# Attention scores in 64x64 array tiles without the masked quarter, and paired half blocks, in a planned attention + MLP kernel

## The chip, the cores and the metric

The kernel runs on one core of a Trainium2 chip. A core has five engines that run side by side and wait for one another through semaphores: TensorE (PE in the profile; its weight loads are shown as PEld), VectorE (DVE), ScalarE (ACT), GpSimd (POOL) and SyncE (SP). POOL, SP and ACT also start DMA transfers. The metric is the device time of one execution in microseconds.

## The reference, cut to what matters

```python
batch, n_heads, seq, head_dim = (8, 8, 576, 64)
scores = scale * np.matmul(q, k.transpose(0, 1, 3, 2))
rel = pos[:, None] - pos[None, :]
bias = slopes[:, None, None] * (-np.abs(rel))[None, :, :]
mask = (rel >= 0) & (rel < 128)
scores = np.where(mask, scores + bias[None], -1000000000.0)
attn = softmax(scores)
x = np.matmul(attn, v) -> (4608, 512)
h = x @ w_in           # 512 -> 2048
g = np.maximum(h, 0.0) ** 2
out = g @ w_out        # 2048 -> 512
```

A query sees itself and the 127 keys before it. Rows 128 to 255 of a batch, as an example, see keys 1 to 255: a block of 128 queries needs its own block of keys and the block before. Cut into quarters of 64 keys by 64 queries, the early half of the earlier keys is outside the window for the late queries, and the late half of the own keys lies in the future of the early queries. So one quarter of each of the two 128x128 squares is masked throughout. A batch of 576 rows is four blocks of 128 and a half block of 64.

## The kernel before, in words

All work is written as tasks, each with the engine (or engines) that may run it, an estimate of its time, what it depends on, and which buffer of which ring it takes and frees. `Plan.order` simulates the engines with these estimates and writes the tasks of each engine in one fixed order. The sort key of a task is a due time plus an adjustment from the table `ADJ` (lines 54 to 444), which holds one number for most tasks; the estimates, `SLACK` (line 27) and the `LAND` times of transfers decide when the planner thinks that a task could start. On the chip each engine then runs its list in that order and waits only where a semaphore says so.

**Loads.** `load_block` (line 819) brings k, q and v of one block from DRAM through POOL's DMA queue, turning them to bf16: k and q into a ring `kq` of 4, v into a ring `vt` of 9 (the blocks that start a batch have places of their own, `vf` and `kqf`). `transpose_kq` (line 893) turns k and q over: for the first 8 blocks by TensorE, for the rest by a DMA transpose on SP's queue into a ring `kqT` of 7. There are 40 blocks: 8 first blocks, 24 full ones and 8 half blocks of 64 rows, and each has a `kq`, a `vt` and a `kqT` buffer of its own, the half blocks too. What the 64 rows of a half block leave free in a buffer is set to zero (`zero`, line 784).

**Scores.** `job` (line 937) makes the scores with keys on the partitions and queries along the row. The head dimension is 64, so a matmul uses 64 rows of the array, and two heads run side by side in its two row halves: the profile writes the tile of the array as `64*128`. A full block takes 16 matmuls of 128 keys by 128 queries (8 heads, two squares). A half job handles the half blocks of two batches together: 32 matmuls of 128 keys by 64 queries, with a 64-query part for each batch. The scores lie in four PSUM banks of the ring `a`. ACT takes the exponential of each bank (`expo`, line 1000: four times 512 columns), DVE multiplies by a table of masks that hold the bias and the window (`mask`, line 1007: four times 512 columns). The result is one buffer of the ring `P` of 3. `place(h)` (line 711) says where a head's part lies. The first four blocks go another way (`lone`).

**Values.** `values` (line 1056) multiplies by v, in two bundles of four heads: 8 matmuls of 128x65 each for a full block (two squares), with a column of ones that gives the sum; DVE takes the reciprocal (line 1108) and scales (line 1117) into a buffer of the ring `x`. In a half job this is done once for each of the two batches, 32 matmuls in all, and each writes half of the partitions of one `x` buffer. A DMA transpose on SP's queue puts `x` into `xT`.

**MLP.** Nine groups of 512 rows. The first product goes through `unit` (line 1227), `fc_step` (line 1252) or, from group 6, a Strassen scheme with seven products (`up_product`, line 1313); ACT and DVE do the squared ReLU. The second is direct for group 0 (`o_piece`, line 1406) and a Strassen scheme from group 1 on (`product`, line 1471). PSUM holds two banks `h`, one each `ox` and `oy`, and four `a`. Attention tasks lie between the MLP's matmuls on TensorE until about two thirds of the time; after that only MLP work is left.

`job` gives the planner's cost of the scores, before the change:

```python
t = plan.add({"PE": 213.0 + len(grps) * 2 * len(pieces) * mm(128 if n == 128 else 64)}, due - 32, scores,
```

## Time and profile before

| what | us |
|---|---|
| median of three runs | 299.22 |
| lowest and highest of them | 297.59, 299.52 |
| the profiled execution | 299.3 |
| its span, first to last instruction | 297.4 |
| PE busy in the span | 285.0 |
| DVE busy | 244.0 |
| ACT busy | 205.8 |
| POOL busy | 106.3 |

The profiled execution took 299.3 us, of which 1.9 us lie outside the span; it stands within 0.1 us of the median. The granted clock of TensorE was 1.00 of full speed. A line of the profile such as `L974 PE MATMUL s<-kqT 64*128 64x128 bf16 x192 | 13.3, 216 | 0.0` says: source line, engine, operation, what it writes and reads, the tile of the array, the shape, how many; then the busy time in us, the mean of one in ns, and the idle time of the engine just before them. A matmul's duration runs from its start to its result, and the next one starts long before that, so what a matmul costs a busy TensorE is the distance between the starts, which the timeline gives, and not the duration.

### The profile page before, as it was taken

The page shows a single profiled execution, that of the slowest core. Times are in us where ns is not written, and L with a number is a line of the kernel's source. Part 1 is how long each engine was busy: PE and PEld are TensorE (multiplying, and loading weights), DVE is VectorE, ACT ScalarE, POOL GpSimd, SP SyncE. Part 2 cuts the span into 40 slices and gives each one's busy share as a digit, 9 for nine tenths or more (in the row PEclk, how much of TensorE's full clock was granted, in tenths as well). Part 3 has the DMA queues.
Part 4 walks back from the last instruction along what each step waited for, and adds up shares of the span by engine and source line. Part 5 has one row for each costly group of instructions (what it writes and reads, how often), then busy time and mean ns, then how long its engine had stood idle before and what let it go on. Part 6 is the DMA issues. An engine that isn't in the chain of part 4 may idle for free.

```text
span 297.4 us, 8313 instructions
## 1 busy us (share of the span) xinstructions
PE 285.0 (96%) x3279; PEld 224.4 (75%) x3299; DVE 244.0 (82%) x626; ACT 205.8 (69%) x392; POOL 106.3 (36%) x132
## 2 busy tenths in 40 slices
PE   7899999999998999899999999999999999999994
PEld 3588757888887986457656756768889888888884
DVE  5566568689976996689958997999999998799964
ACT  2785555495496655877679797878999578989600
POOL 8944488452842755441439622710000000000000
PEclk9999999999999999999999999999999999999999
DMA  9999999999999999999999999998212111201124
GB/s 125 168 201 207 184 180 173 155 157 174 163 165 186 161 146 182 158 165 139 155 186 150 148 191 169 165 130 171 68 40 79 53 35 37 71 2 35 31 77 144
DMA packets 170792, 39.62 MB, mean 133 GB/s; under 512 B 156800, under 2 KB 170240, under 8 KB 170752
## 3 DMA queue, kind: packets, MB, share of 16 engines
q0 software_dynamic: 115184, 18.10, 88.9%
q1 hardware_dynamic: 54768, 20.33, 40.0%
q10 hardware_dynamic: 800, 0.66, 0.8%
q8 instruction: 26, 0.43, 0.6%
q14 instruction: 14, 0.11, 0.1%
HBM read 36.70 MB, written 9.44 MB: 155 GB/s over the span
## 4 chain that ended last, share of the span: by engine, by line
PE 69%; DMA 14%; DVE 6%; POOL 4%; issue 3%; ACT 1%; SPq 0%; POOLq 0%; DVEq 0%
PE o L1503 25%; PE h L1259 12%; PE h L1340 10%; PE h L1241 8%; DMA vt<-in_v_dram 5%; PE o L1416 5%; DMA w_out_sb<-in_moe_w_out_dram 4%; PE pv L1089 4%; PE s L974 4%; DMA kqT<-kq 3%; DMA xT<-x 3%; POOL kq L854 2%; POOL vf L859 1%; DVE g L1214 1%; POOL w_in_sb L799 1%
## 5 line engine op out<-in xcount | busy, mean ns | idle before, releaser
L1202 ACT ACTIVATE rt<-h 128x512 bf16<-128x512 f32 (+1 forms) x109 | 64.8, 597 | 32.8 <-PE h L1241 13.9
L1001 ACT ACTIVATE P<-s 128x512 bf16<-128x512 f32 x120 | 63.8, 604 | 7.8 <-PE s L974 7.7
L1503 PEld LDWEIGHTS <-g 128*128 128x128 bf16 x624 | 59.9, 98 | 8.4
L1214 DVE TENSOR_TENSOR g<-rt 128x512 bf16<-128x512 bf16 (+1 forms) x100 | 41.4, 417 | 20.0 <-ACT rt L1202 18.6
L854 POOL DMA_DIRECT2D kq<-in_k_dram x39 | 33.1, 849 | 66.0 <-DMA kqT<-kq 60.7
L1503 PE MATMUL o<-w_out_sb,g 128*128 128x256 bf16 x384 | 47.5, 273 | 0.0
L1241 PE MATMUL h<-xT,w_in_sb 128*128 128x128 bf16 (+1 forms) x512 | 46.2, 246 | 1.0 <-DMA xT<-x 0.9
L1259 PE MATMUL h<-xT,w_in_sb 128*128 128x512 bf16 x178 | 45.5, 379 | 0.7
L1241 PEld LDWEIGHTS <-w_in_sb 128*128 128x128 bf16 x512 | 38.7, 98 | 5.2 <-issue 1.1
L1009 DVE TENSOR_TENSOR P<-P,masks 128x512 bf16<-128x512 bf16 x96 | 38.4, 417 | 2.5 <-ACT P L1001 0.7
L854 POOL DMA_DIRECT2D kq<-in_q_dram x39 | 33.3, 853 | 7.4 <-PE h L1241 3.1
L1117 DVE TENSOR_TENSOR x<-pv,rec 128x256 bf16<-128x256 f32 (+1 forms) x80 | 32.2, 416 | 0.9
L1503 PE MATMUL o<-wsum,sums 128*128 128x256 bf16 x256 | 31.6, 273 | 1.1 <-DVE osb L1561 0.6
L859 POOL DMA_DIRECT2D vt<-in_v_dram x32 | 27.0, 858 | 11.6 <-PE pv L1089 9.8
L1503 PE MATMUL o<-wsum,g 128*128 128x256 bf16 x240 | 29.8, 273 | 0.1
L1089 PEld LDWEIGHTS <-P 128*128 128x128 bf16 x576 | 24.0, 98 | 7.2 <-issue 2.0
L1259 PEld LDWEIGHTS <-w_in_sb 128*128 128x128 bf16 x192 | 16.9, 97 | 15.9
L1212 ACT ACTIVATE g<-rt 128x512 bf16<-128x512 bf16 x45 | 27.9, 629 | 1.1
L1503 PEld LDWEIGHTS <-sums 128*128 128x128 bf16 x256 | 24.4, 98 | 4.8 <-DVE sums L1633 0.6
L1361 DVE TENSOR_TENSOR vf<-h,vf 128x512 f32<-128x512 f32 x36 | 24.1, 683 | 0.8 <-ACT vf L708 0.4
L1202 ACT ACTIVATE rt<-vf 128x512 bf16<-128x512 f32 x36 | 22.2, 624 | 2.4 <-DVE vf L1361 2.2
L1089 PE MATMUL pv<-vt,P 128*128 128x65 bf16 x448 | 22.0, 193 | 1.3 <-DMA vt<-in_v_dram 1.3
(81 smaller groups left out, 382.0 us busy)
## 6 DMA issues: line engine op xcount, KB each, us to landing
out_dram<-osb SPq DMA_DIRECT2D x53, 128.0 KB, 3.8
kq<-in_k_dram POOLq DMA_DIRECT2D x31, 128.0 KB, 7.6
kq<-in_q_dram POOLq DMA_DIRECT2D x31, 128.0 KB, 7.9
vt<-in_v_dram POOLq DMA_DIRECT2D x24, 128.0 KB, 8.0
w_out_sb<-in_moe_w_out_dram POOLq DMA_DIRECT2D x4, 512.0 KB, 14.7
w_in_sb<-in_moe_w_in_dram POOLq DMA_DIRECT2D x3, 512.0 KB, 10.7
vf<-in_v_dram POOLq DMA_DIRECT2D x8, 128.0 KB, 6.9
out_dram<-osb SPq DMA_DIRECT2D x4, 256.0 KB, 6.4
```

The source lines that it names most:

```text
L854: nc.gpsimd.dma_start(view(kq[s_kq[m].idx], i), source(src, m, split))
L859: nc.gpsimd.dma_start(tile_of(s_v[m])[0:n, :, 0:D], source(v, m))
L1001: nc.scalar.activation(flat(Pt[sP.idx]), sS[i].tile.rearrange("p (j t) -> p j t", j=2)[:, :, lo:hi], AF.Exp, bias=0.0, scale=scale)
L1009: nc.vector.tensor_tensor(flat(Pt[sP.idx]), flat(Pt[sP.idx]), flat(masks), op=ALU.mult)
L1089: nc.tensor.matmul(sv.tile[0:full, hi * (D + 1):(hi + 1) * (D + 1)], prob, tile_of(s_v[mk])[:, h, 0:D + 1], start=mk == parts[0][1], stop= ...
L1117: nc.vector.tensor_tensor(o, heads(sv)[rows, :, 0:D], sr.tile[rows, :].unsqueeze(2).to_broadcast([n, 4, D]), op=ALU.mult)
L1202: nc.scalar.activation(srt.tile[:, 0:n], i, AF.Relu, bias=0.0, scale=1.0)
L1214: nc.vector.tensor_tensor(o, i, i, op=ALU.mult)
L1241: nc.tensor.matmul(slot.tile[:, f * w:(f + 1) * w], w_in_sb[:, cc, fc * 128:(fc + 1) * 128], xT[:, cc, lo % (XR * 128):lo % (XR * 128) + w ...
L1259: nc.tensor.matmul(slot.tile, w_in_sb[:, cc, fc * 128:(fc + 1) * 128], xT[:, cc, g * 512 % (XR * 128):g * 512 % (XR * 128) + 512], start=c ...
L1340: nc.tensor.matmul(slot.tile[:, j * 256:j * 256 + 256], a, b_, start=fresh and j == 0 and c == 0, stop=c == 1, skip_group_check=True)
L1503: nc.tensor.matmul(slot.tile[:, z * 256:z * 256 + 256], stationary(c), moving(c), start=fresh and z == 0 and c == 0, stop=c == F - 1, skip ...
```

## The change

For full blocks, only three of the four quarters of each square are computed, each as matmuls of 64 keys by 64 queries: the output goes to half of the partitions of a bank, so the tile is 64*64 and four can be addressed (two row halves for two heads, two column halves for early and late keys). A full block takes 48 such matmuls in place of 16. Two of the four banks hold 512 columns, two hold 256: the third quarters of the two squares share a bank, one on the early partitions and one on the late. ACT's exponentials are two of 512 and two of 256 columns. DVE's mask instruction for the shared quarters reads 64 columns and writes them twice, each time with a mask that zeroes what belongs to the other square.

The half blocks of two batches become one block of 128 rows: loaded into one `kq` and one `vt` buffer by two transfers of 64 rows for each of k, q and v, turned over by one DMA transpose, and handled as one job with one `x` buffer. There are 36 blocks in place of 40. A half job takes 48 matmuls of 64x64 for the scores in place of 32, a second `P` buffer (`sR`) for the later batch's earlier keys, DVE instructions that mask and clear parts (`clear`, `far_late`, `far_early`, `near`), and 24 value matmuls in place of 32 with one set of reciprocals and scalings in place of two. The instructions that zeroed buffer halves go.

The places of the heads change, planner's estimates change (`S_PE`, the slack of v and x, stores, the landing time of loads), and the `ADJ` table is another, so the order of the work is another. On TensorE the first 503 matmuls stand in the same order as before, past the scores of the first two-block job.

```diff
-SLACK = {"kq": 0.0, "kqT": 4500.0, "v": 2000.0, "x": 2500.0}
+SLACK = {"kqT": 4500.0, "v": 2300.0, "x": 2700.0}
+S_PE = 375.0
...
-        jobs.append(("half", [len(seq), len(seq) + 1]))
-        seq += [(b, HALF), (b + 1, HALF)]
+        jobs.append(("half", [len(seq)]))
+        seq.append((b, HALF))
...
     def place(h):
-        return (h // 4) * 4 + (h % 2) * 2 + (h // 2) % 2
+        return (h % 2) * 4 + h // 2
...
                 for i, src in enumerate((k, q)):
-                    nc.gpsimd.dma_start(view(kq[s_kq[m].idx], i), source(src, m, split))
+                    for rows, from_ in sources(src, m):
+                        nc.gpsimd.dma_start(view(kq[s_kq[m].idx], i)[rows], from_)
...
         if kind == "full":
-            pieces = [(part * 128, 128, part, mk, ms[0]) for part, mk in ((0, before[ms[0]]), (1, ms[0]))]
+            banks = [[(mb, whole, 0, early), (me, whole, 64, late)], [(me, early, 0, early), (mb, late, 0, late)]]
+        elif kind == "half":
+            banks = [[(mk, whole, 64 * i, (early, late)[i]) for i, mk in enumerate(before)],
+                     [(me, early, 0, early), (me, late, 0, late)]]
...
+                todo = [(n, c, p) for n, pieces in enumerate(banks) for c in range(C) for p in pieces]
+                for n, c, (mk, keys, at_c, qs) in todo:
+                    mq = mk if diag else me
+                    for half in (early, late) if keys == whole and not diag else (keys,):
+                        for r in range(2):
+                            rows = slice(64 * r, 64 * r + 64)
...
+                                w = (128, 64)[n]
+                                o = sS[2 * r + n].tile[half, c * w + at_c:c * w + at_c + 64]
+                            nc.tensor.matmul(o, tile_of(s_kqT[mk])[rows, c, half],
+                                             tile_of(s_kqT[mq])[rows, C + c, qs], start=True, stop=True)
...
-            t = plan.add({"PE": 213.0 + len(grps) * 2 * len(pieces) * mm(128 if n == 128 else 64)}, due - 32, scores,
+            t = plan.add({"PE": 213.0 + (449.0 if diag else S_PE)}, due - 32, scores,
...
+            cols = 256 if i % 2 and not diag else 512
...
+                if i % 2:
+                    nc.vector.tensor_tensor(p[:, :, 1:3], p[:, :, 2:3].to_broadcast([128, 4, 2, 64]), mk[:, :, 1:3], op=ALU.mult)
                 else:
+                    nc.vector.tensor_tensor(p[:, :, 0:4:3], p[:, :, 0:4:3], mk[:, :, 0:4:3], op=ALU.mult)
...
+        if kind == "half":
+            def clear():
+                nc.vector.memset(Pt[sR.idx][:, :, 0, early], 0.0)
+
+            def far_late():
+                nc.vector.tensor_tensor(Pt[sR.idx][:, :, 0, late], Pt[sP.idx][:, :, 0, late], masks[:, :, 0, early],
+                                        op=ALU.mult)
+
+            def far_early():
+                p = Pt[sP.idx][:, :, 0, early]
+                nc.vector.tensor_tensor(p, p, masks[:, :, 0, early], op=ALU.mult)
+                nc.vector.memset(Pt[sP.idx][:, :, 0, late], 0.0)
+
+            def near(w):
+                p = Pt[sP.idx][:, w, 1].rearrange("p c (s q) -> p c s q", s=2)
+                nc.vector.tensor_tensor(p, p[:, :, 1:2].to_broadcast([128, 4, 2, 64]),
+                                        masks[:, w, 1].rearrange("p c (s q) -> p c s q", s=2), op=ALU.mult)
+                nc.vector.memset(Pt[sP.idx][early, w, 1, late], 0.0)
...
+            parts = [(s, slice(0, 128), mk) for s, mk in zip((sP, sR), before)] + [(sP, slice(128, 256), m)]
```

## The prediction

> **What bounds the kernel now.** I read the page first.

> ```profile
> span 297.4 us, 8313 instructions
> PE 285.0 (96%) x3279; PEld 224.4 (75%) x3299; DVE 244.0 (82%) x626; ACT 205.8 (69%) x392; POOL 106.3 (36%) x132
> ...
> PEclk9999999999999999999999999999999999999999
> DMA  9999999999999999999999999998212111201124
> ```

> TensorE is the bound: 12.4 us of the span are without a matmul, and the clock is full throughout. DMA is as full, but only up to slice 28, about 208 us; after that TensorE works alone. The view by windows puts the 12.4 us in place.

> ```profile
> 0.00:20.00 20.00, 16.15 (x195) 11.05 (x197) 11.94 (x49) 11.43 (x31) 16.31 (x24) 1.00 1.52 162
> 20.00:280.00 260.00, 255.28 (x2958) 201.26 (x2975) 222.04 (x560) 194.30 (x362) 90.01 (x108) 1.00 1.35 133
> 280.00:298.00 18.00, 13.53 (x132) 12.05 (x130) 10.03 (x18) 0.12 (x1) 0.00 (x0) 0.99 0.33 103
> ```

> The second number of PE is busy time: 3.85 us idle in the start, some 3.9 after 280 us (up to the end at 297.4), and 4.72 in between. So the change can win what it takes off TensorE's list, plus at most a part of these 4.72. Which waits they are, the list of waits says:

> ```profile
> POOL vt L859 <- PE pv L1089: 9.8, 3, 6.8
> ...
> PE pv L1089 <- DMA vt<-in_v_dram: 1.3, 1, 1.3
> ...
> PE h L1241 <- DMA xT<-x: 0.9, 1, 0.9
> ```

> The rest are many small ones. What a score burst costs, the timeline of PE shows by the distance of starts, for a full block (first fence) and for a half job (second):

> ```profile
> 59.37 0.23 PE L974 MATMUL s<-kqT,kqf 64*128 64x128 bf16 x2
> 59.43 0.22 PE L974 MATMUL s<-kqT 64*128 64x128 bf16 x2
> ...
> 59.71 0.22 PE L974 MATMUL s<-kqT,kqf 64*128 64x128 bf16 x2
> 59.77 0.22 PE L974 MATMUL s<-kqT 64*128 64x128 bf16 x2
> ```

> ```profile
> 136.49 0.23 PE L974 MATMUL s<-kqT,kqT 64*128 64x64 bf16 x4
> 136.56 0.22 PE L974 MATMUL s<-kqT 64*128 64x64 bf16 x4
> ...
> 136.91 0.22 PE L974 MATMUL s<-kqT 64*128 64x64 bf16 x4
> ```

> Two matmuls of 128 columns start together every 0.056 us (59.37 to 59.77 in 7 steps, rounded starts; 55.7 ns by the full list). Two of 64 columns start together every 29.2 ns (0.42 us for 14 rounds, so 60 ns for the four of a row). A full burst is 8 rounds, 8 x 55.7 = 446 ns; a half burst 16 x 29.2 = 467 ns. Each is preceded and followed by a gap of about 0.1 us when the array changes its tile (the last row's four end their rounds at 136.97, and the next start is at 137.06).

> **The change, part by part.**

> *Scores.* 24 full and 4 half bursts become 48 matmuls of 64 columns in 64*64 tiles. The trace has no such tile. Lower bound: all four tiles work side by side, 48 / 4 = 12 rounds of 29.2 ns = 350 ns. Upper bound: only two work side by side, as in the half burst now, 24 x 29.2 = 701 ns. In the half burst, two matmuls with their two weight loads are issued within 7 ns of a 29.2 ns round by the full list of starts, so twice as many fit into a round (14 of 29), and issue does not forbid four. Each tile now loads 128 columns of weights per round, afterwards 64. I take 350 ns. Saved: 24 x (446 - 350) + 4 x (467 - 350) = 2304 + 468 = 2.77 us. The gaps around the bursts I leave as they are: the array changes its tile at the same places. A gap twice as long at both ends would cost 28 x 0.2 = 5.6 us; one that vanishes would win as much; the row before me is the same gap for another pair of tiles, so nothing.

> [...] The trace shows only that 128 columns load within 29.2 ns in today's tile.

> *Values.* 32 matmuls go (4 pairs x 8), of 30 ns each:

> ```profile
> 143.13 0.97 PE pv L1089 x32
> ```

> (chain of waits: 0.97 us for 32). Saved: 0.97 us, all on TensorE's path.

> *ACT.* 56 exponentials go from 512 to 256 columns: the 512 form has a mean of 604 ns, the 256 form of the relu has 387, so 56 x 0.217 = 12.2 us less of 205.8. ACT is not the bound; I count nothing. If the strided forms cost 30% more than these rows (56 x 0.18 + 56 x 0.12 = 17 us), ACT would stand at 210 us, far below PE.

> *DVE.* A half job: now four masks (415), four reciprocals (171), four scalings (418) = 4.02 us. Then four masks of 512 columns (417), a cleared half of `P` twice (272 by the memset of 64x256), two small clears (165), two reciprocals and two scalings = 1.67 + 0.54 + 0.33 + 1.18 = 3.72 us. Three memsets of 0.7 us in all go. Together some 2 us less of 244. The new mask form reads one operand twice; the row with a repeated operand (L1016) has 415 ns, the dearest row for 512 columns of DVE has 688. At 688 the 56 instructions would cost 15 us more, 257 of 294: still under PE. Nothing counted, with the cover named: TensorE's other work between scores and values.

> *DMA, SP, POOL.* Bytes are the same, POOL's k, q and v transfers are 78 and 40 as before, SP has 28 transposes of `kqT` in place of 32, the four of them twice as tall. A half pair takes one of nine `vt` and one of seven `kqT` buffers in place of two. The one long wait for v (1.3 us) came from a load that POOL could not start until old values had been used (9.8 us in three waits), so this is eased. I credit 0.5 us, between 0 and the 1.3.

> *Order.* By the order of the built kernel the last score burst has 203.7 us of TensorE work before it (now 200.7, in the same prices), though the attention work before it has become 3.9 us less; so some 6.9 us more MLP work stands ahead of it. Last scores would come at 220.5 + 3.2 = 223.7 us: the loads have more time than today, not less. Nothing counted.

> **Sum.** Against the profiled 299.3 (0.1 over the median): 299.3 - 2.77 - 0.97 - 0.5 = 295.1 us. The start's order is the same and the tail is the same chain, so their 7.7 us stay.

> **The rivals.**

> *New waits at the half blocks (no change).* Values of a half job wait for four exponentials, then for `near`, `far_late`, `far_early`. Order on TensorE gives 5.5, 5.2, 5.2 and 7.7 us of other work between the scores and these values. [...] With 1.0 us lost at each of three such places, and the 0.5 us not won, the time is 295.1 + 3.5 = 298.6. For it: the existing waits on DVE (`osb`, 0.6 us). Against: after the first full blocks today's values follow scores as closely.

> *Tiles that do not work side by side (slower).* If the second column half waits for the first, or a weight load fills more than a round, the burst is up to 701 ns: 24 x 255 + 4 x 234 = +7.06 us, and 299.3 + 7.06 - 0.97 = 305.4. It decides from a round of 40 ns: 28 x 12 x 40 = 13.5 us, what the bursts (12.6) and the values (0.97) cost now. Against it: nothing in today's burst shows the load to be the limit, and per column the load may become twice as slow before it exceeds the round. For it: no row shows that it may not. [...]

> *DMA sets the pace anyway.* Then the saved time turns into waits for `xT`, `kqT` or `vt`. The windows show only 4.7 us of idle under full DMA, and the new order moves the last scores later, so I give it no case of its own; its price is that of the first rival.

> **How the numbers follow.** Forecast 0.58, with its own range from 292 (the 3.7 us, and two thirds of the 4.7 us of waits gone) to 296.2. Waits at the half blocks 0.28, 296.2 to 299.5. Slow tiles 0.12, around 305. Other mishaps of the new order 0.02, slower. Range: 292.0 to 299.5. A measurement here tells about 1% from no change (three runs spread over 1.9 us), so faster means under 296.2: 0.58; within 1%: 0.28; slower: 0.14.

> **What would show it.** In the new timeline the score rows must carry 64*64, four starting together, bursts of about 0.35 us and a step near 29 ns: right for the scores. A step of 40 ns or more: wrong, and the time with it. PE's busy time down by about 3.7 us and its idle time between 20 and 280 us near 4 us: right for the sum. If busy falls and idle rises by as much, with `PE pv` waiting for DVE on lines 1034 to 1046, the first rival holds. Exponentials with 256 columns near 387 ns, and DVE's mask with the repeated operand near 417 ns, check the cover. The forecast is wrong in kind if waits on `vt` or `kqT` grow.

## The result, and the profile after

The changed kernel takes 303.53 us (median of four runs, 302.46 to 307.63), the kernel before 299.37 (four runs beside them, 297.59 to 299.92). The ratio is 1.0138, with an interval of 1.0095 to 1.0181: slower by 1.4%, where 295.1 us and a range of 292.0 to 299.5 had been forecast. Here and below the medians are of all executions of a kernel, and the ratios leave out those that took over 1.5% longer than its fastest. The profiled execution of the changed kernel is the longest of its four runs (307.63 us, of which 305.9 are the span); for sums, a second profile of the same kernel (306.26 us, span 304.5, experiment 1) is used beside it.

The page of the changed kernel, with the rows that answer to those shown of before; the last three give the transfers of instructions (number, MB, share) and the time that a load of k and v takes to land:

```profile
span 305.9 us, 9927 instructions
...
PE 286.6 (94%) x4099; PEld 224.4 (73%) x4099; DVE 238.3 (78%) x621; ACT 196.2 (64%) x394; POOL 106.1 (35%) x132
...
PE   7899999998889999999899999975999999999994
...
PEclk9999999999999999999999999999899999999999
...
q8 instruction: 32, 0.52, 0.7%
...
kq<-in_k_dram POOLq DMA_DIRECT2D x31, 128.0 KB, 10.8
...
vt<-in_v_dram POOLq DMA_DIRECT2D x24, 128.0 KB, 12.4
```

The same rows of before:

```profile
q8 instruction: 26, 0.43, 0.6%
...
kq<-in_k_dram POOLq DMA_DIRECT2D x31, 128.0 KB, 7.6
...
vt<-in_v_dram POOLq DMA_DIRECT2D x24, 128.0 KB, 8.0
```

TensorE is still the bound, but has 19.3 us without a matmul in place of 12.4. In its row of slices the digits below 9 stand at slices 10 to 12, 20, and 27 and 28 (beside start and end), and in slice 29 the clock dips. The view by windows of the changed kernel says the same:

```profile
0.00:20.00 20.00, 16.40 (x196) 11.09 (x197) 11.89 (x49) 11.43 (x31) 16.64 (x25) 1.00 1.53 163
20.00:280.00 260.00, 248.89 (x3706) 194.25 (x3704) 209.59 (x544) 174.35 (x346) 89.51 (x108) 0.99 1.45 133
```

The start is as it was (3.60 us idle in the first 20), and the end nearly so (4.5 us after 280, against 3.9). Between 20 and 280 us TensorE is idle for 11.1 us in place of 4.7. The list of waits of the changed kernel, TensorE's lines:

```profile
PE pv L1119 <- DMA vt<-in_v_dram: 3.1, 1, 3.1
...
PE o L1524 <- issue: 2.5, 2, 1.3
...
PE s L975 <- issue: 1.7, 1, 1.7
PE h L1262 <- issue: 1.7, 1, 1.7
```

One wait is for a load of v, as before but 3.1 us in place of 1.3. The others are new and have no releaser: "issue" is idle time in which no semaphore that the profile shows held the engine back. The timeline shows two of them, the second in the middle of a burst (two cuts of TensorE's timeline):

```profile
73.06 0.22 PE L975 MATMUL s<-kqT,kqf 64*64 64x64 bf16 x4
73.11 0.20 PE L975 MATMUL s<-kqT 64*64 64x64 bf16 x4
73.14 0.20 PE L975 MATMUL s<-kqT,kqf 64*64 64x64 bf16 x4
...
73.30 0.23 PE L975 MATMUL s<-kqT 64*64 64x64 bf16 x6
...
73.43 0.20 PE L975 MATMUL s<-kqT,kqf 64*64 64x64 bf16 x2
73.56 0.28 PE L1524 MATMUL o<-wsum,sums 128*128 128x256 bf16 x1
75.06 0.82 PE L1524 MATMUL o<-wsum,sums 128*128 128x256 bf16 x6 [1.21 <-issue]
```

```profile
201.79 0.19 PE L975 MATMUL s<-kqT 64*64 64x64 bf16 x1
203.65 0.19 PE L975 MATMUL s<-kqT 64*64 64x64 bf16 x1 [1.67 <-issue]
203.66 0.22 PE L975 MATMUL s<-kqT,kqf 64*64 64x64 bf16 x2
```

A burst itself is of the kind that the forecast named: 64*64, four together, six rounds from 73.11 to 73.30, 31.6 ns each by the full list of starts (the first of a burst takes 52 ns). But in the second fence two matmuls of one burst, with the same operands in place, stand 1.86 us apart. There are six such steps in this execution, 7.6 us in all. Counted over the rows of TensorE (matmuls, weight loads and some 20 rows of semaphores, 8200 in all, against 6600 before), each falls on the same place of a block of 256: numbers 1985, 2241, 2497, 4545, 5825 and 6081, all 193 above a multiple of 256. And 32 transfers of 16,384 bytes for 8200 rows, 26 for 6600, is one for every 256 rows. The trace's list of DMA packets gives the start and end of each. The table below has times in us, in the changed kernel; its last two columns are the same blocks in experiment 7, in which most k, q and v loads are a quarter as long. Some traces lack matmul rows (20 of 4099 in experiment 7, 20 of 3299 before); there the blocks are counted by the weight loads, of which none is missing.

```
first row   packet    packet  the block   packet's end    step   exp. 7: packet's   exp. 7:
of block    starts    ends    begins      to begin               end to begin       step
1985         72.36     73.65    75.06        1.40          1.38        2.60           none
2241         80.70     81.84    83.34        1.50          1.46        4.20           none
2497         88.49     90.32    92.01        1.68          1.83        4.97           none
2753         96.90     97.83   100.63        2.80          none        6.33           none
4545        153.55    155.64   157.04        1.41          0.72        5.16           none
5825        193.64    194.71   196.09        1.38          0.31        5.20           none
6081        200.84    202.11   203.65        1.54          1.86        3.78           none
```

A step ends 1.38 to 1.68 us after the packet's end, whatever its length; where the packet ends 1.8 us or more ahead there is none in this execution. Before the change, blocks between 60 and 205 us lasted 8.5 to 14.7 us, and every packet there had landed at least 4.6 us ahead, though it started up to 4.4 us after the block before had begun. After the change the blocks last 5.9 to 10.2 us, and the packets start up to 5.6 us after the block before has begun: the room has gone, mostly because the blocks are shorter.

Before the change TensorE's list of waits has 0.2 us of "issue" in all, on line 1416, and no such step at the end of a block; here six block ends cost 7.6 us.

### The profile page after: what moved, and what is told of

The parts are those of the page before. It is cut to its first block, busy times and chain, and to the rows that moved or that the text cites. A ratio compares the mean times of both kernels' runs of the same rounds, so it can differ in the third digit from the quotient of the medians.

```text
span 305.9 us, 9927 instructions
## 1 busy us (share of the span) xinstructions
PE 286.6 (94%) x4099; PEld 224.4 (73%) x4099; DVE 238.3 (78%) x621; ACT 196.2 (64%) x394; POOL 106.1 (35%) x132
## 3 DMA queue, kind: packets, MB, share of 16 engines
q0 software_dynamic: 115184, 18.10, 89.6%
## 4 chain that ended last, share of the span: by engine, by line
PE 75%; DMA 14%; DVE 5%; issue 2%; ACT 2%; SPq 0%; POOL 0%; POOLq 0%; DVEq 0%
PE o L1524 25%; PE h L1262 12%; PE h L1361 12%; PE h L1280 11%; DMA xT<-x 6%; PE o L1437 4%; PE pv L1119 4%; DMA vt<-in_v_dram 4%; PE s L975 4%; DMA kqT<-kq 3%; DMA wsum<-in_q_dram 2%; DVE sums L1653 1%; PE tp L913 1%; DVE g L1235 1%; ACT rt L1223 1%
## 5 line engine op out<-in xcount | busy, mean ns | idle before, releaser
L1524 PEld LDWEIGHTS <-g 128*128 128x128 bf16 x624 | 59.8, 98 | 10.2 <-issue 1.6
L1008 ACT ACTIVATE P<-s 128x512 bf16<-128x512 f32 (+1 forms) x120 | 51.8, 503 | 18.3 <-PE s L975 18.0
L1235 DVE TENSOR_TENSOR g<-rt 128x512 bf16<-128x512 bf16 (+1 forms) x105 | 43.7, 419 | 23.4 <-ACT rt L1223 21.7
L1524 PE MATMUL o<-w_out_sb,g 128*128 128x256 bf16 x384 | 48.9, 276 | 0.0
L859 POOL DMA_DIRECT2D vt<-in_v_dram x32 | 26.8, 849 | 21.9 <-PE pv L1119 6.2
L713 ACT ACTIVATE osb<-o 128x512 f32<-128x512 f32 x25 | 14.8, 599 | 29.0 <-PE o L1524 24.9
L1119 PEld LDWEIGHTS <-P 128*128 128x128 bf16 x544 | 23.0, 98 | 8.7 <-issue 4.6
L1143 DVE TENSOR_TENSOR x<-pv,rec 128x256 bf16<-128x256 f32 x72 | 28.4, 415 | 0.6
L1233 ACT ACTIVATE g<-rt 128x512 bf16<-128x512 bf16 x40 | 25.2, 630 | 1.2
L1119 PE MATMUL pv<-vt,P 128*128 128x65 bf16 x416 | 21.0, 194 | 3.7 <-DMA vt<-in_v_dram 3.1
## 6 DMA issues: line engine op xcount, KB each, us to landing
kq<-in_q_dram POOLq DMA_DIRECT2D x31, 128.0 KB, 11.1
vt<-in_v_dram POOLq DMA_DIRECT2D x24, 128.0 KB, 12.4
```

Source lines behind the costliest of these rows:

```text
L859: nc.gpsimd.dma_start(tile_of(s_v[m])[rows, :, 0:D], from_)
L1008: nc.scalar.activation(o, s, AF.Exp, bias=0.0, scale=scale)
L1119: nc.tensor.matmul(sv.tile[:, hi * (D + 1):(hi + 1) * (D + 1)], prob, tile_of(s_v[mk])[:, h, 0:D + 1], start=mk == parts[0][2], stop=mk == m)
L1143: nc.vector.tensor_tensor(o, heads(sv)[:, :, 0:D], sr.tile.unsqueeze(2).to_broadcast([n, 4, D]), op=ALU.mult)
L1233: nc.scalar.activation(o, i, AF.Square, bias=0.0, scale=1.0)
L1235: nc.vector.tensor_tensor(o, i, i, op=ALU.mult)
```

## The experiments

Two theories stand against each other. Theory I: TensorE runs out of instructions, since the attention stage issues more of them per us, and their transfers come late behind the traffic of the loads. Theory W: the time went into waits for data that the new order of work makes late; the number of instructions by itself costs nothing. Experiments 1 to 4 were compared with 13 runs of the kernel before (median 299.38), 5 to 8 with 22 (299.35).

**1. The changed kernel again**

> The changed kernel as it is, to have its profile beside the others. Theory I (instructions): TensorE's instructions come in blocks of 256 by a transfer of 16 KB each; where a block is used up before the next has come, TensorE stands. In the profile of the changed kernel six steps of 0.41 to 1.94 us without a releaser lie at instruction numbers that are all 193 modulo 256. It expects such steps here again, 3 to 8 us in all, each ending 1.4 to 1.7 us after the end of an instruction transfer, in a time of 302 to 304 us. Theory W (waits of the new order): the time is lost in waits for vt, xT and kqT (4.3 us in that profile); it expects 4 us or more of these and under 1.5 us of steps without a releaser.

Measured: 306.19 us (305.39 to 309.23), ratio 1.0253 (1.0176 to 1.033), above the 302 to 304 expected and above the 303.53 of the first result, by the same kernel. TensorE's list of waits in it:

```profile
PE o L1524 <- issue: 3.3, 3, 2.7
PE pv L1119 <- DMA vt<-in_v_dram: 2.7, 1, 2.7
PE s L975 <- issue: 1.9, 1, 1.9
```

The steps are at block ends again, but not at the same six: 2.87 us at 73.76, 2.13 at 200.97 and three short ones, 6.3 us together. Which block ends cost something differs between the two profiles, and the time of this kernel between the two sets of executions, 303.53 and 306.19 us. Against before, the span is 7.1 us longer: +6.3 (steps), +1.4 (the wait for v, 2.82 us between starts in place of 1.42), +3.1 (the granted clock is 0.5 for 3.41 us each from 76.06 and 212.59, at the stalls of 2.87 and 2.82 us; an estimate, half of the 2.74 and 3.41 us that lie behind them), and -2.3 of work (below). That is 8.5; the other -1.4 us were not followed one by one, but before's waits of TensorE for `osb` (0.6 us), `P` (0.4) and `w_out_sb` (0.4) are not among those of this execution. So both theories have a part: I the steps, W the wait for v.

**2. The same tiles, fewer instructions**

```diff
-                    for half in (early, late) if keys == whole and not diag else (keys,):
+                    for half in (keys,):
```

The two wide quarters of a square go in one matmul of 128 keys: 32 matmuls per burst in place of 48, 28 instruction transfers in place of 32.

> The changed kernel in the same order of work, but each matmul with 128 keys stays whole (tile 64*128, 64 columns), so a burst is 32 matmuls in place of 48: bank 0 in 8 rounds of 29.2 ns, bank 1 in 4 rounds of 31.6 ns, and one more change of the tile, 0.46 us in place of 0.38: 28 x 0.08 = 2.2 us more matmul work, 896 instructions fewer. Theory I: a block of 256 lasts 10% longer, the steps at block ends fall to under 2 us in all, and the time is 299 to 302 us. Theory W: 2 us more than the changed kernel, 305 us.

Measured: 303.12 us (301.53 to 304.36), ratio 1.0129 (1.0062 to 1.0196). No step at a block end is left, as theory I said; the time is above its range. What is left is the wait for v, and with it a spell of half the clock at 209.04; experiment 6 takes both away:

```profile
PE pv L1119 <- DMA vt<-in_v_dram: 3.1, 1, 3.1
PE h L1280 <- DMA xT<-x: 1.8, 2, 0.9
```

**3. The kernel before, with its score matmuls cut into two halves of the keys**

```diff
-                            for r in range(2):
...
+                            for hk in (slice(0, 64), slice(64, 128)) if kind != "diag" else (slice(0, 128),):
+                                for r in range(2):
```

> The kernel before in its order, with each score matmul split into two of 64 keys (64*64 tiles, the same columns, all four quarters computed): 1024 instructions more, and bursts of the same rounds (8 of about 56 to 60 ns in a full block, 16 of 31.6 in a half job): at most 0.5 us more matmul work. Theory I: blocks of 256 pass some 20% faster where attention is, some ends of blocks come too early: 300 to 304 us, with steps without a releaser at one place modulo 256. Theory W: no change, 299.5 us.

Measured: 303.18 us (10 runs, 300.31 to 308.5), ratio 1.0122 (1.0079 to 1.0164). The time is theory I's, but the profiled execution happens to be the fastest of the ten (300.31) and has no step at a block end; its waits are two for `xT`. For the cause this run is inconclusive.

**4. The kernel before, with its score matmuls cut into quarters of 64x64, all four computed**

```diff
+                            for q0, hk in [(q0, hk) for q0 in range(0, w, 64) for hk in (slice(0, 64), slice(64, 128))] if kind != "diag" else [(0, slice(0, 128))]:
...
+                                    nc.tensor.matmul(sS[2 * g2 + r].tile[hk, jj * 256 + c0 + q0:jj * 256 + c0 + q0 + qw],
+                                                     tile_of(s_kqT[mk])[rows, c, hk], tile_of(s_kqT[mq])[rows, C + c, q0:q0 + qw],
```

The order of the work, the loads and the half blocks are those of before; only the number of instructions on TensorE grows, by 2560.

> The kernel before in its order, with each score matmul of a full block split into four of 64 keys by 64 queries, and of a half job into two (64*64 tiles, all four quarters computed): 2560 instructions more. Bursts of 16 rounds of 31.6 ns, 505 ns in place of 446: 24 x 0.06 + 4 x 0.04 = 1.6 us more matmul work. Theory I: blocks last 6 to 8 us where attention is, ten or more of them end early by 0.5 to 2 us: 306 to 316 us. Theory W: 301 us.

Measured: 310.67 us (309.51 to 311.76), ratio 1.0389 (1.0312 to 1.0466). There are four steps of 1.0 to 2.5 us at block ends, where ten or more were expected, with no wait for v, and two spells of half the clock. The steps are 7.3 of the 11.0 us by which the span is longer; the longer bursts (0.668 us from their first start to the next one behind them, against 0.553 and 0.573) are 3.1. One of the steps, in its timeline, splits a group of eight:

```profile
96.05 0.19 PE L976 MATMUL s<-kqT,kqf 64*64 64x64 bf16 x1
98.55 0.25 PE L976 MATMUL s<-kqT,kqf 64*64 64x64 bf16 x7 [2.31 <-issue]
```

The steps come with the instructions, without the new order: theory W does not explain them.

**5. The changed kernel, with two loads of v exchanged**

```diff
+    i, j = (next(n for n, t in enumerate(done) if t.name == f"lv{m}") for m in (34, 32))
+    done[i], done[j] = done[j], done[i]
+    s_v[34].idx, s_v[32].idx = s_v[32].idx, s_v[34].idx
```

The wait for v has one place. The view of the lines that load v, in the profile of experiment 1 and from 190 to 213 us, shows the last loads and who waits for them:

```profile
L859 POOL DMA_DIRECT2D vt<-in_v_dram x5: 734/878/885, 190.1 to 197.7; - x5
...
  PE pv L1119: 2.7, 1
...
DMA to landing us min/median/max: 9.5/11.4/13.8
```

Five loads are left at 190 us, and the last is issued at 197.7. It brings block 32, which TensorE needs at 208.7, before those of the loads issued ahead of it. In the kernel before, the last five were issued from 179.4 to 193.6 and landed within 4.3 to 7.7 us, in time. Here the load of block 32 changes places (and buffers) with that of block 34.

> The changed kernel with one swap on POOL's queue: of the last three loads of v, the one whose values TensorE needs first comes first and not last (buffers swapped too); every other engine's order is the same. Theory I (instructions come too late) together with W (a wait for vt of 2.8 to 3.3 us late in attention, after which the granted clock is 0.5 for 3.4 us, 1.7 us more): the vt wait and the clock dip after it go, the steps at block ends stay: 4.5 us less than the changed kernel, 299 to 302 us. If the wait for vt only follows from the steps before it, or the next load is as late: no change, 303 to 306 us.

Measured: 303.33 us (10 runs, 299.82 to 307.14), ratio 1.0084 (1.0033 to 1.0135), above the range expected. The profiled execution is the slowest of the ten (307.14 us). No wait of TensorE for v is left in it; the steps stay, in its list of waits, as they do in experiment 1:

```profile
PE o L1524 <- issue: 5.2, 3, 3.2
PE s L975 <- issue: 2.2, 1, 2.2
PE h L1280 <- DMA xT<-x: 1.8, 1, 1.8
```

**6. Both edits, of experiments 2 and 5**

> Matmuls with 128 keys kept whole (896 instructions fewer than the changed kernel) and the swap of the last loads of v. Theories I and W: neither steps at block ends nor the late vt wait, which leaves about 2 us of waits for xT: 303.1 - 4.5 = 298.6 us, level with the kernel before or somewhat faster. If another wait takes its place: 302 to 303 us.

Measured: 298.19 us (10 runs, 295.35 to 301.36), ratio 0.9944 (0.9899 to 0.999): as expected, and faster than either kernel, if only by half a per cent against the one before, with an interval that ends just under 1. The page of the profiled execution (296.74 us):

```profile
span 295.0 us, 9013 instructions
...
PE 284.8 (97%) x3633; PEld 224.1 (76%) x3651; DVE 238.3 (81%) x621; ACT 196.2 (67%) x394; POOL 106.2 (36%) x132
...
PE   7799999999999999999999899999999999999994
...
PEclk9999999999999999999999999999999999999999
```

No step at a block end and no wait for v; the longest wait after the start is 1.0 us for `xT`. Each edit alone leaves the kernel slower than before, both together make it slightly faster. This holds although its burst, with the array's tile changed once more inside, takes 0.59 us from its first start to the next one behind it, where the change has 0.51 (73.06 to 73.56). What the slower executions of this kernel (up to 301.36 us) still wait for was not seen.

**7 and 8. Short loads, in the changed kernel and in the one before**

The lines of the changed kernel (the first for k and q, the second for v); the kernel before has the same cut in its own:

```diff
+                        n_rows = (rows.stop - rows.start) // (4 if m >= 8 else 1)
...
+                n_rows = (rows.stop - rows.start) // (4 if m >= 19 else 1)
```

From block 8 on for k and q, and from block 19 on for v, only a quarter of the rows is loaded, so the results of these blocks are not the reference's. All other work is done, with the same number of instructions.

> The changed kernel with little DMA traffic: from block 8 on, k and q are loaded for a quarter of the rows only, from block 19 on v too (the rest of a buffer keeps older values, so the output is not the reference's); transposes, stores and the order of work are as in the changed kernel. Theory I in the form that instruction transfers are late because they queue behind data transfers: they come on time, no steps at block ends, waits for vt and xT gone: 292 to 296 us. If TensorE can't be supplied faster whatever the traffic (the rate alone): the steps stay, 298 to 302 us.

> The kernel before with the same cut of the loads (a quarter of the rows; the output is not the reference's): its 3.0 us of waits for transfers go, 296 to 297 us. The changed kernel with this cut should then be 2 to 4 us faster than this one, by its shorter matmul work; by the rate alone it would be 2 us slower or more.

Measured: 293.76 us for the changed kernel (293.63 to 294.21; ratio 0.9828, 0.9777 to 0.9879), 296.59 for the one before (296.35 to 297.1; ratio 0.992, 0.9896 to 0.9944). The page of the first:

```profile
span 292.0 us, 9909 instructions
...
PE 282.8 (97%) x4079; PEld 223.6 (77%) x4099; DVE 237.6 (81%) x621; ACT 195.9 (67%) x394; POOL 83.7 (29%) x132
...
PE   7799999999999999999999999999999999999993
...
q8 instruction: 32, 0.52, 0.7%
```

With the same 32 transfers of instructions, no step is left. As the table above shows, each packet now ends 2.6 us or more ahead of its block; it starts 0.1 to 1.4 us after the begin of the block before, where under full traffic it starts 3.4 to 5.6 us after (same six blocks). So TensorE can run at this rate of instructions; what fails is that the transfers come late while the loads of k, q and v fill the DMA (queue q0 moves 18.10 MB with a share of 89.6% in the first profile, 10.92 MB with 47.6% here). And the change by itself, without this disturbance, is worth 293.76 - 296.59 = -2.83 us, where the work taken off TensorE had been put at 3.74. Work accounts for 2.3 of the 2.83 (below); of the rest it is known only that the kernel before, with short loads, still has 1.0 us of waits of TensorE for `osb` and `P`, which the changed kernel has not.

What stays open: only starts and ends of the instruction transfers are seen, not what asks for them or where they queue; and which block ends cost how much in an execution that isn't profiled, so any step of experiment 3 in its slower executions was not seen.

## Why the prediction was wrong

*Scores: right in kind, off in size, and one cost was missing.* The tiles are 64*64, four at a time, and the gap ahead of a burst is as it was (0.203 us from start to start, 0.205 before). But a round takes 31.6 ns in place of 29.2, and the first of a burst 52. From the first start of a burst to the next one behind it TensorE now takes 0.509 us, where it took 0.553 for a full block and 0.573 for a half job. So the saving is 24 x 0.044 + 4 x 0.064 = 1.3 us, not 2.77. That still speaks against the rival of tiles that do not work side by side: 31.6 ns is under its point of 40.

The step that failed is "issue does not forbid four". It was drawn from one round: twice as many matmuls fit into 29 ns. That was true within a burst, as the rounds show. But 1600 more instructions on TensorE were priced at nothing in the sum, and they meet a second limit, their transfer in pieces of 16 KB: it cost 6.3 us of steps in experiment 1 and 7.6 in the first profile. The row of before that bore on it, q8 with 26 transfers, was on the page and had not been used.

*Values: right.* 32 matmuls fewer at 30 ns: 0.97 us. With the 1.3 of the scores that is 2.3 us of work, where the sum had 3.74.

*ACT and DVE: right.* The exponentials have 391 ns with 256 columns (387 forecast), the mask with the repeated operand 417 (417); ACT falls from 205.8 to 196.2, DVE from 244.0 to 238.3; these sums also hold seven copies to `osb` that moved from DVE to ACT and five squares of the ReLU that moved the other way. No wait of TensorE on lines 1034 to 1046 is in its list: the rival of waits at the half blocks did not come, and no run shows the 1.0 us at each of three places that it was priced with.

*DMA and order: wrong.* "The loads have more time than today, not less" was argued from the last score burst, which does come later (234.9 us in experiment 1, against 220.9 before; 223.7 was forecast, and the step to it is 203.7 - 200.7 = 3.0 us, not the 3.2 that it adds). It says nothing of values: POOL issues the load that is needed first of the last ones as the last, and the time to land grew from 8.0 to 12.4 us at the median, and POOL's waits for old values are 9.8 us in experiment 1, as before. So the credit of 0.5 us for an eased wait became a loss of 1.4, with a spell of half the clock behind it. "I give it no case of its own; its price is that of the first rival" is the second step that failed: that DMA sets the pace was the case that came, in a form that its price did not hold.

*The test named for the sum.* PE's busy time did not fall by 3.7 us but rose from 285.0 to 286.6 (286.1 in experiment 1), and the idle time between 20 and 280 us rose by 6.4. Busy time was a poor test here, since matmuls at half the clock count as busy (four `h<-ut,kqf` of line 1361 for 1.06 us at 214.80 in the first profile, in the spell, and for 0.61 at 216.47, behind it); with short loads, where the clock stays full, it falls from 284.3 to 282.8.

## What to carry to other kernels

Before cutting matmuls into smaller ones, count the instructions on TensorE per us: see how much shorter a block of 256 of them will become, and compare this with the margin by which the instruction transfers land ahead of their blocks today. Where the DMA is full and little of that margin would be left, expect stalls at some block ends: here blocks of 8.5 to 14.7 us, with a margin of 4.6 us or more, had none, and of those of 5.9 to 10.2 us six had one, of 0.31 to 1.86 us. Two edits that each lose can win together when each removes a stall of its own, so measure the stalls and not only the total. After an order is changed, follow each late load to its first user in POOL's order of issue; the last burst of one kind of work says nothing of the others.
